# Moving VectorE work behind a copy, and re-dealing background steps, in a fused attention and two-MLP kernel

## The chip, the cores and the metric

The kernel runs on one core of a Trainium2 chip. The metric is device time in microseconds, as the median of several runs; lower is better.

## The reference

Eight batches (B = 8) of eight heads, 576 rows of 64, go through a packed attention: 32 packed queries p attend to k and v, and then q attends to the packed result, which serves as key and value.

```
s = scale * q @ k.T ; a = exp(s - max(s)) ; a = a / (sum(a) + 1e-9) ; out = a @ v
p_packed = attention(p, k, v)
out      = attention(q, p_packed, p_packed)
x = out as 4608 x 512
x = silu(x @ w_in1) @ w_out1            # 512 -> 2048 -> 512
x = (h * clip(h + 3, 0, 6) / 6) @ w_out2, h = x @ w_in2
```

All is float32 at the ends. Products are made exact enough by splitting each operand in a high and a low part (gh and gl, a2h and a2l, and so on) and adding three products.

## The kernel before, in words

The 4608 tokens are worked in NBLK = 9 blocks of 512: blocks 0 to 7 hold the first 512 rows of each batch, block 8 the 64-row tails of all eight. `block` (L985) runs the first MLP on one block: for each of 16 slices f of the inner dimension it calls `hidden` (L937: the products into hps, then Silu on ScalarE), `split_g` (L963: gh on ScalarE, gl on VectorE), and `projects(f - 2)` (L997 and L970: 12 products into four accumulators). Blocks 0 and 8 are fat: their hidden part has 12 products per f; in the others the attention's value product is folded into the weights and it has 6. After the ninth block a second MLP (`Second`, L1056) works on everything.

**The attention is threaded between these products.** Half a batch (four heads) is a quad n; 16 quads. A `window(c, d, b, a, ...)` (L823) lists steps for four quads in different stages: c is in its first softmax's scores, d in its second softmax's, b is c of the window before, a is d of the window before. `Plan` (L753) holds the steps with a place in the block, a list of needs and a wait in ticks; a tick is one matmul of the MLP. `tick` runs, between products, each step whose place has come and whose needs are met, in the order of places. Every engine carries out its instructions in the order in which they are issued, and so does the DMA queue of SyncE.

The steps that matter here, in the order of places in a window:

- `exps` (L834) and `ends` (L839) of the window before: the two exponentials on ScalarE, and after them `post1(b)` (L459, the reciprocal of the first softmax's sum) and `post2(a)` (L562, four VectorE instructions L566 to L569: sum, add, reciprocal, multiply of the second softmax's weights).
- `t`: `step_kpq` (L398) transposes the first softmax's weights of b and the tails of k and q on TensorE and copies them out: a1 by ScalarE, a1Tt and qtT by VectorE (L111 is the helper's line), kp by ScalarE.
- `pp` (L489; L466 has the products): the first softmax's weights times v. It reads a1 (L472) and a1Tt (L475). In block 1 it is a step of its own, 6 ticks or more after `t`; later it is part of the score step.
- `q0, q1, k0, k1` (`turn`, L859; `step_tr`, L442): from quad 4 on each is one VectorE transpose (L446) of a loaded tile nat. They need nothing of the `t` step. The second of each pair calls `use`, which may issue the next loads.
- `u` (L571 and L580): VectorE transposes the scaled weights (L573, and the tails, L585) and splits them.
- the score step (`step_zs`, L508): L514 reads q, L518 reads k, L608 reads the tails. It also ends the use of v, upon which the loads of the next v, q and k are issued.

Block 1 has the windows (c, d) = (4, -), (5, -), (6, 4), (7, 5), and a closing window without new quads. A window is named here by this pair; b = 5 and a = none in (6, 4), b = 6 and a = 4 in (7, 5), b = 7 and a = 5 in the closing one. Blocks 2 to 5 have two windows with quads and a closing one; block 6 none with a new c; block 7 none.

**Preparation.** Beside this, `Prep` (L269) turns the second MLP's weights into seven combinations in DRAM, in 32 units of nine steps after six empty ones (L313 to L343). A unit's stages: two ScalarE passes over the loaded tile praw (L180, L186), two VectorE passes (L195, L199) with the load of the next unit's tile issued a step later (L289, L291), a GpSimd add (L324), four VectorE sums (L327 to L330), two ScalarE copies (L332, L333), two GpSimd subtractions (L335, L336) and, with the next unit's first step, three stores on SyncE's queue (L340 to L342). `nxt` (L1879) runs the steps. It is called with full = True after `split_g` and at the end of an f, and with full = False in the middle of the projects (from f = 2 on) and, in a fat block, in the middle of the hidden part. In blocks 1 to 6 a call with full = True runs one step and one with False none; in block 7 (j == B - 1) two and one; in block 8 one and none.

```
1889    for _ in range(1 + full if j == B - 1 else full):
1890        prep.step()
```

Of the kernel before, what the change touches and what calls it, by code (L numbers as in the profile page):

```python
# [18 lines left out]
def tile_pack_attention_two_mlps(ctx: ExitStack, tc, q, k, v, p, w_in1, w_out1, w_in2, w_out2, out):  # L19
# [9 lines left out]
    B, H, S, D = q.shape  # L29
# [368 lines left out]
    def step_kpq(c, d, b, p=None, x=None):  # L398

        if b is not None:  # L400
            d1, _ = st.pop(("d1", b))
            rows = bank()
            for i in range(NI):
                nc.tensor.transpose(rows[:, i * P:(i + 1) * P], d1[:, i * P:(i + 1) * P], ident)
        ps = bank()
        if b is not None:
            nc.tensor.transpose(ps[0:TAIL, 3 * P:], d1[:, T:S], ident)
        if p is not None:
            step_pt(p)
        if x is not None:  # L410
            step_xt(x, ps[:, 3 * P:])
        if c is not None:
            nc.tensor.transpose(ps[:, 0:P], pair(st.pop(("pbd", c)), 0), ident)
        for a, what, n in (1, "k", c), (2, "q", d):
            for j in range(2 if n is not None else 0):
                o = a * P + j * TAIL
                nc.tensor.transpose(ps[:, o:o + TAIL], pair(nat[what, n], j), ident[0:TAIL, 0:TAIL])
            if n is not None:
                del nat[what, n]
        if b is not None:  # L420
            st["a1", b] = half_kb(b, "T", 5)
            copy(out=st["a1", b], in_=rows)
            st["a1t", b] = at.tile([TAIL, P], F32, tag="a1Tt", name="a1Tt")
            copy_short(out=st["a1t", b], in_=ps[0:TAIL, 3 * P:])
        if p is not None:
            step_ptc(p)
        if c is not None:
            t = at.tile([P, 2 * P], F32, tag="kp", name="kp")
            copy(out=t, in_=ps[:, 0:2 * P])
            st["kp", c] = t  # L430
        if d is not None:
            t = at.tile([P, P], F32, tag="qtT", name="qtT")
            copy_short(out=t, in_=ps[:, 2 * P:3 * P])
            st["qt", d] = t
        if x is not None:
            step_xtc(x)
# [5 lines left out]
    def step_tr(n, what, j):  # L442
        m = nat.pop((what, n, j))
        if n >= 4:
            t = half_kb(n, "T", 5)
            nc.vector.transpose(out=t, in_=m)  # L446
            st[what, n, j] = t
            return
        ps = bank()
        turn_rows(ps, m)  # L450
        t = half_kb(n, "T", 5)
        copy(out=t, in_=ps)
        st[what, n, j] = t
# [260 lines left out]
    for j in range(2, B - 1):  # L714
        c, d = QPB * (j + 2), QPB * (j + 1)
# [107 lines left out]
    def window(c, d, b, a, j, x):  # L823
# [4 lines left out]
        before = ("exps", b, a), ("ends", b, a)  # L828

        def add(n, what, cost, fn, *need, tile=None, bank=5, also=(), count=1):  # L830
            if n is not None:
                steps.append(((what, n), cost, fn, need, tile, bank, [k for k in also if k[1] is not None], count))
# [4 lines left out]
                    fn(n)  # L837

        def ends():  # L839
            for n, fn in (c, post1), (d, post2):  # L840
                if n is not None:
                    fn(n)

        def kpq():
            step_kpq(c, d, b)
            if c is not None:
                load_p_after(c)

# [6 lines left out]
        if ends_block:  # L855
            a = None
        add(c, "spread", 0, lambda: spread_p(c), ("kpq", b), bank=0)

        def turn():  # L859
            add(d, "q0", 0, lambda: step_tr(d, "q", 0), bank=0, tile=("z", d))  # L860
            add(d, "q1", 0, lambda: [step_tr(d, "q", 1), use("q", d)], ("q0", d), bank=0, tile=("z", d))
            add(a, "u", 0, lambda: [step_u(a), step_ut(a)], before[1], bank=8)
            add(c, "k0", 0, lambda: step_tr(c, "k", 0), (("q1", d), 0), bank=0, tile=("s", c))
            add(c, "k1", 0, lambda: [step_tr(c, "k", 1), use("k", c)], ("k0", c), bank=0, tile=("s", c))

# [13 lines left out]
        else:  # L879
# [2 lines left out]

            def transposes():
                step_kpq(c, d, b, p0, x)
                if c is not None:
                    load_p_after(c)

# [30 lines left out]
        steps.append((("ends", c, d), 0, ends, (("exps", c, d),), None, 0, (), 1))  # L918
        return steps

    pend = []

    WAIT = {"spread": 8, "kpq": 7, "q0": 6, "q1": 8, "k0": 6, "k1": 8, "t": 8, "tt": 8, "pp": 9, "pt": 6, "z": 4, "zt": 10, "s": 4, "st": 7,
            "exps": 22, "ends": 18, "u": 14, "split": 10, "xt": 12}
# [905 lines left out]
    for j in range(NBLK):  # L1830
# [46 lines left out]
        calls = [0]  # L1877

        def nxt(f, full, j=j):  # L1879
            if j == 0:  # L1880
                if full:
                    feed.advance()
                    calls[0] += 1
                    if 20 <= calls[0] < 25:
                        next_in()
                else:
                    feed.begin()
            else:
                for _ in range(1 + full if j == B - 1 else full):
                    prep.step()  # L1890
                if full and j == B:
                    mlp2.begin_step()

        def boundary(j=j):
            if j < B - 1:
                n = QPB * (j + 2) - 1
                plan.finish(lambda key: key[0] == "ends" and key[2] == n)
                step_u(n)
                step_ut(n)
            elif j == B - 1:  # L1900
                for c in range(KC):
                    split_x(c, xf[c])
# [44 lines left out]
```

## Time and profile before

| | |
|---|---|
| runs | 1529.72, 1538.01, 1539.9 us; median 1538.01 |
| profiled execution | 1529.94 us, its span 1528.1 us, mean granted TensorE clock 0.996 |
| TensorE matmul | 1482.3 us busy, 97% of the span |
| VectorE, ScalarE, GpSimd | 1034.6, 778.8, 190.8 us busy |
| blocks 0, 1, 7, 8 of the first MLP | 151.8, 110.8, 76.5, 85.6 us |
| blocks 2 to 6 together | 406.3 us |
| second MLP | 697.1 us |

A block is measured from the last copy of the block before's accumulators (L1028) to its own. PE is TensorE, PEld its weight loads, DVE VectorE, ACT ScalarE, POOL GpSimd, SP SyncE; SPq is its DMA queue. A matmul's recorded duration is longer than its distance to the next, since matmuls overlap; distances are taken from starts. In brackets at the end of a timeline row stands the idle time of the engine just before it and what ended it.

### The profile page before, as it was taken

What the parts mean: (1) busy time and instruction counts of PE and PEld (TensorE: products, weight loads), DVE (VectorE), ACT (ScalarE), POOL (GpSimd) and SP (SyncE); (2) the same over time, 40 slices, a digit from 0 to 9 for tenths busy, and PEclk for the clock granted to TensorE, in tenths of its full rate; (3) what the DMA queues carried; (4) which work ended last, traced back from release to release, by engine and by line L of the source; (5) the groups of instructions that cost most, each with busy time, mean ns of one, the idle gap of its engine ahead of it and who ended that gap; (6) DMA issues with size and microseconds to landing.
All of it is one profiled execution on the core that took longest, in us unless ns stands there. A gap on an engine that the chain in (4) does not pass through costs nothing.

```text
span 1528.1 us, 21726 instructions
## 1 busy us (share of the span) xinstructions
PE 1482.3 (97%) x7550; PEld 1229.2 (80%) x7550; DVE 1034.6 (68%) x1695; ACT 778.8 (51%) x1241; POOL 190.8 (12%) x177
## 2 busy tenths in 40 slices
PE   7999978999999999999999999999999999999998
PEld 4777756777777777777788888888888888999998
DVE  6767456765576656644452768877887787878777
ACT  6876646655575466555442334433443344444442
POOL 2433101111211211124220000000000000000000
PEclk9999999999999999999999999999999999999999
DMA  9998788978598759859893667677767766897887
GB/s 246 313 308 283 217 220 229 276 210 226 158 261 249 204 140 318 241 162 270 239 285 120 195 207 233 194 221 235 234 193 221 233 218 209 282 315 253 271 274 222
DMA packets 434509, 358.52 MB, mean 235 GB/s; under 512 B 191200, under 2 KB 325856, under 8 KB 434400
## 3 DMA queue, kind: packets, MB, share of 16 engines
q1 hardware_dynamic: 423632, 343.79, 76.0%
q10 hardware_dynamic: 10768, 13.34, 2.7%
q8 instruction: 61, 1.00, 0.3%
q14 instruction: 48, 0.39, 0.1%
HBM read 295.17 MB, written 61.87 MB: 234 GB/s over the span
## 4 chain that ended last, share of the span: by engine, by line
PE 81%; DMA 6%; DVE 4%; ACT 4%; SPq 2%; issue 1%; POOL 1%; ACTq 0%; POOLq 0%; DVEq 0%
PE b L1223 8%; PE b L1224 8%; PE b L1222 8%; PE b L1317 7%; PE b L1320 7%; PE b L1319 7%; PE acc L974 7%; PE acc L975 7%; PE acc L976 7%; PE hps L951 4%; PE hps L953 4%; PE hps L952 4%; DMA nat<-in_k_dram 1%; DMA w1i<-win 1%; DMA wi<-w1i 1%
## 5 line engine op out<-in xcount | busy, mean ns | idle before, releaser
L967 DVE TENSOR_TENSOR gl<-hps,gh 128x512 fp32r<-128x512 f32 x144 | 98.8, 686 | 173.8 <-ACT gh L966 173.4
L1319 PE MATMUL b<-ro,ws 128*128 128x512 f32 (+2 forms) x564 | 206.2, 366 | 0.0
L1320 PE MATMUL b<-ro,ws 128*128 128x512 f32 (+2 forms) x564 | 206.2, 366 | 0.0
L1222 PE MATMUL b<-xc,ws 128*128 128x512 f32 (+1 forms) x560 | 205.6, 367 | 0.0
L1224 PE MATMUL b<-xc,ws 128*128 128x512 f32 (+1 forms) x560 | 205.6, 367 | 0.0
L1223 PE MATMUL b<-xc,ws 128*128 128x512 f32 (+1 forms) x560 | 205.5, 367 | 0.0
L1265 DVE TENSOR_TENSOR ro<-g,ro 128x1024 fp32r<-128x1024 f32 (+1 forms) x140 | 161.3, 1157 | 41.6 <-ACT ro L1260 41.3
L1260 ACT CAST ro<-g 128x1024 fp32r<-128x1024 f32 (+1 forms) x140 | 132.0, 967 | 93.3 <-DVE g L1253 33.3
L1317 PE MATMUL b<-ro,ws 128*128 128x512 f32 (+2 forms) x564 | 138.9, 367 | 0.3
L959 ACT ACTIVATE hps<-hps 128x512 f32<-128x512 f32 x144 | 84.2, 584 | 99.7 <-PE hps L953 98.9
L974 PE MATMUL acc<-gh,wo 128*128 128x512 f32 x288 | 116.1, 403 | 2.8 <-ACT gh L966 2.8
L1319 PEld LDWEIGHTS b<-ro,ws 128*128 128x128 f32 x564 | 105.9, 188 | 13.2
L1320 PEld LDWEIGHTS b<-ro,ws 128*128 128x128 f32 x564 | 105.9, 188 | 13.1
L1222 PEld LDWEIGHTS b<-xc,ws 128*128 128x128 f32 x560 | 105.1, 188 | 13.3
L1223 PEld LDWEIGHTS b<-xc,ws 128*128 128x128 f32 x560 | 105.1, 188 | 13.2
L1224 PEld LDWEIGHTS b<-xc,ws 128*128 128x128 f32 x560 | 105.1, 188 | 13.0
L974 PE MATMUL acc<-gh,wr 128*128 128x512 f32 x288 | 113.7, 395 | 1.8 <-ACT gh L966 1.8
L1317 PEld LDWEIGHTS b<-ro,ws 128*128 128x128 f32 x564 | 102.9, 188 | 15.1 <-DVE ro L1265 2.2
L975 PE MATMUL acc<-gl,wo 128*128 128x512 f32 x288 | 113.7, 395 | 0.6 <-DVE gl L967 0.4
L976 PE MATMUL acc<-gh,wo 128*128 128x512 f32 x288 | 113.4, 394 | 0.0
L975 PE MATMUL acc<-gl,wr 128*128 128x512 f32 x288 | 112.7, 391 | 0.5 <-DVE gl L967 0.4
L976 PE MATMUL acc<-gh,wr 128*128 128x512 f32 x288 | 112.4, 390 | 0.0
(310 smaller groups left out, 2887.5 us busy)
## 6 DMA issues: line engine op xcount, KB each, us to landing
ws<-w2in SPq DMA_DIRECT2D x280, 256.0 KB, 3.3
ws<-w2out SPq DMA_DIRECT2D x280, 256.0 KB, 3.4
wi<-w1i SPq DMA_DIRECT2D x80, 512.0 KB, 6.2
wo<-w1o SPq DMA_DIRECT2D x64, 512.0 KB, 5.8
x1d<-x SPq DMA_DIRECT2D x18, 512.0 KB, 5.3
w1i<-win SPq DMA_DIRECT2D x16, 512.0 KB, 6.4
praw<-in_moe_w_in_dram SPq DMA_DIRECT2D x32, 256.0 KB, 5.5
praw<-in_moe_w_out_dram SPq DMA_DIRECT2D x32, 256.0 KB, 5.8
```

What stands on the lines that cost most here:

```text
L967: nc.vector.tensor_sub(out=gl, in0=g, in1=f32(gh))
L974: mm(acc[e], lhsT=w[:, 0, s], rhs=gh, start=first, stop=False)
L975: mm(acc[e], lhsT=w[:, 0, s], rhs=gl, start=False, stop=False)
L976: mm(acc[e], lhsT=w[:, 1, s], rhs=gh, start=False, stop=last)
L1222: mm(ps, lhsT=wh, rhs=xs[k][:, 0, c], start=first, stop=False, skip_group_check=True)
L1223: mm(ps, lhsT=wh, rhs=xs[k][:, 1, c], start=False, stop=False, skip_group_check=True)
L1224: mm(ps, lhsT=wl, rhs=xs[k][:, 0, c], start=False, stop=last, skip_group_check=True)
L1260: nc.scalar.copy(out=t[:, 0], in_=v)
L1265: nc.vector.tensor_sub(out=t[:, 1], in0=self.operand(s), in1=f32(t[:, 0]))
L1317: mm(to, lhsT=wh, rhs=x, start=False, stop=last, skip_group_check=True)
L1319: mm(to, lhsT=wh, rhs=x, start=first, stop=False, skip_group_check=True)
L1320: mm(to, lhsT=wl, rhs=x, start=False, stop=False, skip_group_check=True)
```

## The change

Three things. The transposes of q and k in block 1 also need `t` of the same window (in other blocks the added need names a step that does not exist and is always met). `ends` no longer scales the second softmax's weights where the window has a c: it notes d in the list `after_t`, and `weigh` scales what is noted, at the end of `t`'s own work, or at once where there is no c, or at the block's boundary before u; u needs `t` as well. And a call of `nxt` in blocks 7 and 8 runs one preparation step whatever full is, in block 7 every sixth call two; in blocks 1 to 6 nothing changes there.

```diff
         def ends():
-            for n, fn in (c, post1), (d, post2):
-                if n is not None:
-                    fn(n)
+            if c is not None:
+                post1(c)
+            if d is not None:
+                after_t.append(d)
+            if c is None:
+                weigh()
 
         def kpq():
             step_kpq(c, d, b)
+            weigh()
...
         def turn():
-            add(d, "q0", 0, lambda: step_tr(d, "q", 0), bank=0, tile=("z", d))
+            add(d, "q0", 0, lambda: step_tr(d, "q", 0), (("t", b if j == 1 else None), 0), bank=0, tile=("z", d))
             add(d, "q1", 0, lambda: [step_tr(d, "q", 1), use("q", d)], ("q0", d), bank=0, tile=("z", d))
-            add(a, "u", 0, lambda: [step_u(a), step_ut(a)], before[1], bank=8)
+            add(a, "u", 0, lambda: [step_u(a), step_ut(a)], before[1], (("t", b), 0), bank=8)
             add(c, "k0", 0, lambda: step_tr(c, "k", 0), (("q1", d), 0), bank=0, tile=("s", c))
...
             def transposes():
                 step_kpq(c, d, b, p0, x)
+                weigh()
...
-    pend = []
+    pend, after_t = [], []
+
+    def weigh():
+        while after_t:
+            post2(after_t.pop(0))
...
             else:
-                for _ in range(1 + full if j == B - 1 else full):
+                calls[0] += 1
+                for _ in range(1 + (j == B - 1 and calls[0] % 6 == 0) if j >= B - 1 else full):
                     prep.step()
...
                 plan.finish(lambda key: key[0] == "ends" and key[2] == n)
+                weigh()
                 step_u(n)
```

## Rows read from the trace of the kernel before

**Rows 1.** Page: the chain of waits, shares of the span by engine.

```profile
PE 81%; DMA 6%; DVE 4%; ACT 4%; SPq 2%; issue 1%; POOL 1%; ACTq 0%; POOLq 0%; DVEq 0%
```

**Rows 2.** Busy time by stretch: blocks 1, 2 to 6, 7, 8; length, engines, clock, DMA.

```profile
151.80:262.60 110.80, 98.47 (x600) 74.89 (x599) 58.34 (x127) 59.90 (x100) 13.99 (x17) 0.98 0.79 216
262.60:668.90 406.30, 400.48 (x2142) 316.12 (x2141) 263.64 (x534) 244.80 (x415) 68.20 (x67) 1.00 0.79 222
668.90:745.40 76.50, 70.81 (x294) 55.26 (x293) 33.73 (x73) 42.02 (x74) 32.43 (x27) 0.98 0.92 247
745.40:831.00 85.60, 85.60 (x379) 70.87 (x378) 30.61 (x45) 31.88 (x51) 11.26 (x8) 1.00 0.73 219
```

**Rows 3.** Timeline of TensorE, block 1: start, duration, line, operation, tiles, count, idle.

```profile
173.11 0.32 PE L475 MATMUL abank<-vt,a1Tt 64*32 64x64 f32 x8 [1.09 <-DVE a1Tt L111]
...
196.58 0.44 PE L475 MATMUL abank<-vt,a1Tt 64*32 64x64 f32 x8 [4.49 <-DVE a1Tt L111]
196.95 0.80 PE L974 MATMUL acc<-gh,wo 128*128 128x512 f32 x1
...
199.68 0.45 PE L951 MATMUL hps<-a2h,fused 128*128 128x512 f32 x1
...
225.30 0.32 PE L475 MATMUL abank<-vt,a1Tt 64*32 64x64 f32 x8 [2.71 <-DVE a1Tt L111]
...
232.84 0.39 PE L608 MATMUL abank<-tails,ppf 128*128 128x128 f32 x2
...
249.18 0.32 PE L475 MATMUL abank<-vt,a1Tt 64*32 64x64 f32 x8 [1.86 <-DVE a1Tt L111]
```

**Rows 4.** Busy time by stretch, behind the stop at 196.58.

```profile
196.60:200.00 3.40, 3.40 (x16) 2.60 (x17) 1.46 (x4) 1.46 (x3) 0.00 (x0) 0.53 0.88 309
```

**Rows 5.** Timeline of VectorE in window (6, 4).

```profile
192.07 0.71 DVE L446 STREAM_TRANSPOSE T<-nat 128x512 f32<-128x512 f32 x1 [2.25 <-DMA nat<-in_q_dram]
...
196.26 0.26 DVE L111 COPY a1Tt<-abank 64x128 f32<-64x128 f32 x1
...
197.64 0.71 DVE L446 STREAM_TRANSPOSE T<-nat 128x512 f32<-128x512 f32 x1 [0.38 <-DMA nat<-in_k_dram]
```

**Rows 6.** Timeline of VectorE in window (7, 5).

```profile
221.56 0.71 DVE L446 STREAM_TRANSPOSE T<-nat 128x512 f32<-128x512 f32 x1 [1.51 <-DMA nat<-in_k_dram]
...
223.02 0.73 DVE L566 TENSOR_REDUCE s2s<-d 128x18 f32<-128x576 f32 x1
...
224.97 0.28 DVE L111 COPY a1Tt<-abank 64x128 f32<-64x128 f32 x1
...
228.39 0.49 DVE L585 STREAM_TRANSPOSE tails<-d 64x64 f32<-64x64 f32 x2
```

**Rows 7.** Timeline of VectorE in the closing window of block 1.

```profile
246.87 0.97 DVE L567 TENSOR_SCALAR s2s<-s2s 128x18 f32<-128x18 f32 x1
```

**Rows 8.** TensorE's waits in block 7: us in total, times, longest.

```profile
PE acc L974 <- ACT gh L966: 4.6, 4, 2.6
```

**Rows 9.** ScalarE's waits in block 7.

```profile
ACT hi L332 <- POOL c L324: 16.0, 8, 3.3
ACT pr L180 <- DMA praw<-in_moe_w_out_dram: 10.9, 4, 4.0
```

**Rows 10.** ScalarE's longest wait in block 8.

```profile
ACT hps L959 <- PE hps L953: 36.3, 13, 4.2
```

**Rows 11.** Timeline of SyncE's queue, the loads of q for window (7, 5).

```profile
206.96 7.25 SPq L373 DMA_DIRECT2D nat<-in_q_dram  x8
```

**Rows 12.** Timeline of ScalarE, gh in window (7, 5).

```profile
220.82 0.59 ACT L966 CAST gh<-hps 128x512 fp32r<-128x512 f32 x1
```

**Rows 13.** TensorE's waits for a1Tt in blocks 2 to 6.

```profile
PE abank L475 <- DVE a1Tt L111: 0.8, 1, 0.8
```

**Rows 14.** Page: DMA issues, preparation's loads: count, KB each, us to landing.

```profile
praw<-in_moe_w_out_dram SPq DMA_DIRECT2D x32, 256.0 KB, 5.8
```

**Rows 15.** Waits of SyncE's queue in block 7.

```profile
SPq L340 <- ACT hi L333: 27.8, 6, 14.4
```

## The prediction

> **What bounds the kernel now.** I read the chain of waits first: TensorE holds 81% of it, every other engine or queue 6% or less [rows 1]. So time can only come from places where TensorE stands still or runs slowly, and the next view is the busy time by stretch, block by block [rows 2]. The reader is to compare the length of a stretch with TensorE's busy time in it. Block 8 has no idle time: 85.60 us for 379 matmuls, 0.226 us each. Blocks 2 to 6 lose 5.8 us in 406. Block 1 loses 12.3 us in 110.8, and block 7, with less to multiply than block 8, loses most per microsecond: 294 matmuls at block 8's 0.226 us are 66.4 us, and the block takes 76.5, so 10.1 us are lost (5.7 idle, the rest matmuls that run slower around the stops). These two blocks are the ones that the change works on.
>
> In block 1 TensorE stops at one instruction, L475, which multiplies by the copied tail of the first softmax's weights (a1Tt): 1.09, 4.49, 2.71 and 1.86 us in its four windows [rows 3]. After the long stop the granted clock is 0.53, the lower of its two levels (1.2 of 2.4 GHz), for 3.4 us [rows 4]. VectorE's rows say why a1Tt is late. In window (6,4) VectorE sits in front of transposes of q and k whose data are still under way (2.25 us at 192.07) and copies a1Tt only at 196.26, behind them [rows 5]. In window (7,5) the same transposes end at 222.27, and then the second softmax's scaling (L566 to L569) runs from 223.02 to 224.97, ahead of the copy [rows 6]. In the closing window the scaling alone stands there [rows 7].
>
> In block 7 TensorE waits for gh, a ScalarE product, 4.6 us in four stops [rows 8]. ScalarE is late because the preparation's steps block it: it waits 10.9 us for the preparation's loads, up to 4.0 at a time, and 16.0 us for GpSimd's add [rows 9]. In block 8, where the preparation runs at two steps per f, ScalarE instead waits 36.3 us for TensorE [rows 10]: it has time to spare.
>
> **The change part by part.** *Transposes of q and k in block 1.* They now need the step t of the same window. That binds in windows (6,4) and (7,5) alone, since the others have no q. Four L446 of 0.71 us each [rows 5] move behind t's copies, with the two calls that may issue loads. Those calls issue nothing where they stand: the next loads wait for v, released in the score step, and the queue spends 7.25 us on q's eight transfers alone after that [rows 11]. So nothing moves on SP's queue or POOL's.
>
> Window (6,4): t's matmuls stay where they are, and VectorE goes from gl straight to a1Tt. What is left of the 4.49 us lies between 0 and 1.09, the stop in the window that has neither transposes nor scaling in front [rows 3]; gl, which waits for ScalarE, still stands ahead of the copy, so I take 0.4. Gain 4.1. The slow stretch goes too: from 196.95 to 199.68 six matmuls take 2.73 us [rows 3], 1.36 at 0.226; gain 1.4. Together 5.5 (4.8 to 5.9). Behind the moved transposes queue the next gl, the value product's scaling and the splits of fused weights. The last transpose starts at 197.64 because its data land then [rows 5]; without the stop the scores come some 5.5 us before their old place, still just after it. I charge nothing here; if that cover is gone, the score step waits, which is a rival below.
>
> Window (7,5): 2.71 falls to 0.5 by the same bounds, gain 2.2 (1.6 to 2.7). Here something is late next: step u, whose tails end at 228.88 [rows 6] and are read by L608 at 232.84 [rows 3]. With VectorE free for gl at 221.41, when gh ends [rows 12], and not when the k transpose lets go, and with four transposes (2.8 us) in front, they end near 228.9 - 0.8 + 2.8 = 230.9; L608 will want them near 230.6. I charge 0.5 (0 to 2.0). Net 1.7 (-0.4 to 2.7).
>
> *The scaling behind the copies.* It is off the path until u. In the closing window 1.86 us go; the work behind the copy (scaling, value, u, splits into block 2) is as long as before and ends hardly sooner, so I keep 1.2 (0 to 1.86). Block 1 in all 8.4 (4.4 to 10.5). In block 0 the copies are ScalarE's, and windows without a next k scale where they did: nothing. In blocks 2 to 6 one stop of 0.8 us at L475 is all there is to win [rows 13]: 0.6 (0 to 0.8). The new wait of u for t adds nothing, since u already waits 18 ticks behind the ends step that comes before t.
>
> One row speaks against moving the scaling: its 18-element L567 took 0.97 us in the closing window, half of the 1.95 us that the whole group took in the window before [rows 6, 7]. The Trainium skill (SBUF — State Buffer, Who interferes with whom) says that VectorE and GpSimd share one port pair which an instruction holds to its end, so a moved scaling that meets a preparation add waits for all of it. By that rule the sum would be smaller by one such wait of 0.8 us, in window (7,5), 16.7 instead of 17.5. The row agrees with a wait of this kind but does not name GpSimd.
>
> *Preparation.* Calls per block are counted from the code: in block 7, 46 (two for each of the first two f, then three), before 32 x 2 + 14 x 1 = 78 steps, now 46 + 7 = 53; in block 8, before 32, now 62. Blocks 1 to 6 give 192 either way, and all units need 295. So before 25 steps were left for block 8, now 50; both end near its f = 12. About 2.8 units of nine steps leave block 7, with their loads, ScalarE passes, GpSimd adds and stores. In block 7 a unit's load and its first use are six steps apart: before a little over one f (4.1 us at 18 matmuls), now two f, 8.2 us, against 5.8 us from issue to landing [rows 14]. So ScalarE's wait for loads should vanish, and with at most one of a unit's chained stages in most f the 16.0 us behind GpSimd shrink. Of 10.1 us I take 9.0 back (5 if the start of the block, with stores and loads crowded, stays as it is; 10.1 at most).
>
> Block 8 takes 25 more steps. Priced as in block 7, 10.1 / 78 = 0.13 us each, they would cost 3.3 us; hidden they cost nothing. I take 0.5, nearest the row of this block itself: 36.3 us of ScalarE waiting and no TensorE idle time [rows 2, 10]. DMA there rises from 219 GB/s (18.7 MB) by 2.8 x 1.4 MB (512 KB in and 896 out per unit, by the code) to some 267 GB/s, share 0.89 by proportion, below block 7's 0.92 [rows 2].
>
> **Sum.** 8.4 + 0.6 + 9.0 - 0.5 = 17.5 us (6 to 21.4). The profiled execution took 1529.94 us, so 1512.4 (1508.5 to 1524). The median of the runs shown is 1538.01, 8.1 above it, and no row tells where the 8.1 lie; halfway between 1512.4 and 1520.5 I predict 1516.
>
> **Rivals.** *A: block 7 goes on stopping*, because the loads are late through traffic and not through spacing (DMA share 0.92 there [rows 2]). For it: the first stops would stand at the block's start, where stores of block 6 land too. Against: blocks 2 to 6 run the same chain at two steps per f with hardly a stop. Then only 8.5 us go: about 1521 in the profile. Chance 0.11. *B: the wait moves to the scores.* The transposes come late, L514 and L518 stop instead of L475, and block 1 gives nothing: 1529.9 - 9.1 = 1521. For it: k's last data in window (6,4) land at 197.64 [rows 5] whatever the order. Against: the scores come after that. Chance 0.11. *C: slower, by block 8.* SP's queue is in order; in block 7 a preparation store at its head waited up to 14.4 us for ScalarE [rows 15]. If stores of the five units now in block 8 hold the weights' loads back like this, TensorE waits for wi. With five tiles a load has some four f of 5.4 us, so it decides only from a delay of about 15 us on; 1.1 us in each of the 16 f eats the gain, 2.2 us gives 35 - 17 = 18 us slower, 1548. Against: ScalarE is rarely late in block 8 [rows 10]. Chance 0.06. *D: the change does not bind*: if t is emitted early anyway, order stays as it was; but the rows show the copies last in all three windows. Chance 0.02, 1538.
>
> **Numbers.** The forecast has 0.70. 1% (15.4 us; about what a measurement of this kernel can tell from no change) lies inside its spread: I put 0.53 of it on faster by over 1% and 0.17 within. A and B give 0.05 faster and 0.17 within, C 0.05 slower and 0.01 within, D 0.02 within; 0.58, 0.37, 0.05. The range runs from 1507 to 1531: the sum's upper end below, A and B with the runs' 8.1 us above.
>
> **What would show it.** Right: L475's stops in block 1 under 1 us each, a1Tt ahead of L566 and of the L446 pair, no stretch at a granted clock near 0.5 there; block 7 near 67 us with ScalarE's wait for praw near nothing; block 8 still at 0.226 us per matmul. Wrong: stops at L514, L518 or L608 in windows (6,4) and (7,5); gh still late in block 7; TensorE waiting for wi or gh in block 8.

## The result and the profile after

The changed kernel takes 1518.54 us (median of six runs, 1516.09 to 1520.86) beside 1535.12 for the kernel before (1529.72 to 1539.9): ratio 0.989, 95% interval 0.987 to 0.992. A second measurement gave 0.990 (0.988 to 0.991). The forecast was 1516. The profiled execution took 1516.09 us, its span 1514.3.

In the chain of waits TensorE's share is 86%, against 81% in [rows 1], and every other engine has 4% or less.

Busy time by stretch, in the columns of [rows 2]: block 1, blocks 2 to 6, block 7, block 8.

```profile
152.40:258.70 106.30, 99.48 (x597) 75.12 (x596) 57.31 (x126) 59.39 (x99) 14.01 (x17) 0.98 0.83 225
258.70:665.50 406.80, 401.30 (x2143) 316.39 (x2142) 264.72 (x534) 245.13 (x416) 68.25 (x67) 1.00 0.80 223
665.50:730.60 65.10, 65.10 (x290) 53.90 (x289) 28.29 (x59) 35.45 (x62) 21.77 (x18) 1.00 0.84 222
730.60:817.20 86.60, 86.60 (x384) 71.71 (x383) 38.04 (x60) 38.47 (x64) 23.84 (x17) 1.00 0.89 260
```

Against [rows 2]: block 1 is 4.5 us shorter, blocks 2 to 6 are 0.5 longer, block 7 is 11.4 shorter and block 8 1.0 longer. Block 0 is 0.6 longer, and the second MLP takes 697.1 us as before. In all 13.85 us.

**Block 7 has no idle time left.** ScalarE's waits there (us in total, times, longest) answer to [rows 9]: 16.0 us behind GpSimd's add and 10.9 for praw have become these.

```profile
ACT hi L332 <- POOL c L324: 0.7, 1, 0.7
ACT pr L180 <- DMA praw<-in_moe_w_out_dram: 0.6, 1, 0.6
```

Block 8's extra 1.0 is no slowing: it has 384 matmuls instead of 379, still at 0.226 us each, and block 7 has 290 instead of 294. The copy that makes the border was VectorE's before and ended at 745.37, 2 us behind block 8's first product; it now comes some four matmuls earlier. Blocks 7 and 8 together went from 162.1 to 151.7.

**In block 1 L475 waits in one window only, the one the change does not touch, and two other waits of about a microsecond or more have appeared.** Timeline of TensorE, as in [rows 3]. The first row is window (5, -). Lines from the f-loop on stand nine further down, so L974 is now L983.

```profile
173.72 0.32 PE L475 MATMUL abank<-vt,a1Tt 64*32 64x64 f32 x8 [1.08 <-DVE a1Tt L111]
...
192.72 0.32 PE L475 MATMUL abank<-vt,a1Tt 64*32 64x64 f32 x8
...
217.86 0.32 PE L475 MATMUL abank<-vt,a1Tt 64*32 64x64 f32 x8
...
225.97 0.64 PE L518 MATMUL abank<-T,kp 128*64 128x512 f32 x1 [0.95 <-DVE T L446]
...
241.78 0.32 PE L475 MATMUL abank<-vt,a1Tt 64*32 64x64 f32 x8
...
249.67 0.50 PE L983 MATMUL acc<-gh,wo 128*128 128x512 f32 x1 [2.40 <-DMA wo<-w1o]
```

TensorE's waits at L472 for ScalarE's copy a1, 2.1 us in three stops, are the same before and after.

VectorE's rows show the order that the change asked for. The first two are window (6, 4): the copy, and the last of the four transposes of q and k behind it, late with its data; compare [rows 5].

```profile
192.40 0.26 DVE L111 COPY a1Tt<-abank 64x128 f32<-64x128 f32 x1
...
199.29 0.71 DVE L446 STREAM_TRANSPOSE T<-nat 128x512 f32<-128x512 f32 x1 [3.57 <-DMA nat<-in_k_dram]
...
217.54 0.26 DVE L111 COPY a1Tt<-abank 64x128 f32<-64x128 f32 x1
...
218.45 0.74 DVE L566 TENSOR_REDUCE s2s<-d 128x18 f32<-128x576 f32 x1
...
222.75 0.69 DVE L573 STREAM_TRANSPOSE abank<-d 128x512 f32<-128x512 f32 x1
...
225.21 0.71 DVE L446 STREAM_TRANSPOSE T<-nat 128x512 f32<-128x512 f32 x1
```

The last four rows are window (7, 5): copy, then scaling, then u from 222.75. The last transpose of k comes at 225.21, behind u, and it is what L518 waits for at 225.97.

The second new wait is a load. SyncE's queue around it:

```profile
233.01 5.42 SPq L373 DMA_DIRECT2D nat<-in_q_dram  x8
238.53 5.33 SPq L373 DMA_DIRECT2D nat<-in_k_dram  x8
243.96 0.57 SPq L260 DMA_DIRECT2D wo<-w1o  x1
```

The load of wo is issued at 243.96, directly behind sixteen loads of q and k that hold the queue without a gap (in the trace of before it was issued at 244.50). TensorE now wants it at 247.27 and gets it at 249.67. Then the clock falls to its lower level for part of the next stretch (clock 0.62 in this row):

```profile
250.00:254.50 4.50, 4.50 (x14) 3.53 (x13) 0.43 (x1) 1.52 (x3) 0.00 (x0) 0.62 1.03 341
```

Fourteen matmuls at 0.226 us would be 3.2 us; they take 4.5.

### The profile page after: what moved, and what is told of

It reads as the page before. It is cut to its first block, busy times and chain, and to the rows that moved or that the text cites. A ratio compares the mean times of both kernels' runs of the same rounds, so it can differ in the third digit from the quotient of the medians.

```text
span 1514.3 us, 21726 instructions
## 1 busy us (share of the span) xinstructions
PE 1477.9 (98%) x7550; PEld 1227.8 (81%) x7550; DVE 1036.3 (68%) x1695; ACT 778.8 (51%) x1241; POOL 192.5 (13%) x177
## 4 chain that ended last, share of the span: by engine, by line
PE 86%; ACT 4%; DMA 4%; DVE 3%; issue 1%; SPq 1%; POOL 0%; ACTq 0%; DVEq 0%; POOLq 0%
PE b L1232 8%; PE b L1233 8%; PE b L1231 8%; PE b L1326 8%; PE acc L983 8%; PE b L1329 7%; PE b L1328 7%; PE acc L984 7%; PE acc L985 7%; PE hps L960 4%; PE hps L962 4%; PE hps L961 4%; PE abank L672 1%; DMA w1i<-win 1%; PE abank L674 1%
## 5 line engine op out<-in xcount | busy, mean ns | idle before, releaser
L968 ACT ACTIVATE hps<-hps 128x512 f32<-128x512 f32 x144 | 84.1, 584 | 97.5 <-PE hps L962 96.7
L983 PE MATMUL acc<-gh,wo 128*128 128x512 f32 x288 | 115.3, 400 | 2.4 <-DMA wo<-w1o 2.4
L983 PE MATMUL acc<-gh,wr 128*128 128x512 f32 x288 | 113.5, 394 | 0.0
```

The source lines that it names most:

```text
L983: mm(acc[e], lhsT=w[:, 0, s], rhs=gh, start=first, stop=False)
```

## The experiments

Each was profiled once and timed against the kernel before on the same chip. The ratio is taken over all runs; the lengths in us, by the same borders, are those of one execution:

| kernel | ratio (95%) | block 1 | block 2 | 3 to 6 | 7 | 8 |
|---|---|---|---|---|---|---|
| before | | 110.8 | 83.6 | 322.7 | 76.5 | 85.6 |
| changed | 0.989 (0.987 to 0.992) | 106.3 | 84.0 | 322.8 | 65.1 | 86.6 |
| after_again | 0.990 (0.988 to 0.991) | 107.3 | 84.1 | 324.7 | 65.2 | 86.5 |
| e1_prep_only | 0.993 (0.991 to 0.995) | 116.2 | 84.1 | 323.2 | 65.1 | 86.6 |
| e2_transposes_only | 0.996 (0.995 to 0.998) | 109.0 | 84.2 | 323.3 | 76.7 | 85.6 |
| e3_scaling_only | 0.995 (0.993 to 0.997) | 106.0 | 84.3 | 323.0 | 77.0 | 85.5 |
| e4_wo_scalar_queue | 0.990 (0.988 to 0.992) | 103.0 | 91.2 | 323.5 | 65.2 | 86.5 |
| e5_transposes_together | 0.988 (0.986 to 0.990) | 106.1 | 88.5 | 324.9 | 65.1 | 86.7 |
| e8_both | 0.988 (0.986 to 0.990) | 104.0 | 87.9 | 323.7 | 65.1 | 86.6 |
| e6_before_early_loads | 1.000 (0.999 to 1.002) | 112.1 | 83.6 | 323.6 | 77.8 | 84.0 |
| e7_loads_before_stores | 0.996 (0.994 to 0.997) | 115.5 | 86.8 | 322.6 | 69.9 | 85.7 |
| e9_prep_off_block1 | 0.997 (0.996 to 0.999) | 99.8 | 83.9 | 344.6 | 65.2 | 87.4 |
| e10_prep_off_wo_scalar | 0.998 (0.997 to 1.000) | 99.8 | 82.9 | 344.8 | 65.2 | 87.6 |
| e11_less_prep_in_block1 | 0.994 (0.992 to 0.995) | 101.3 | 90.7 | 336.0 | 63.7 | 86.5 |

### One part at a time

**The preparation alone** (the kernel before, with the two lines of the dealing).

```diff
-                for _ in range(1 + full if j == B - 1 else full):
+                calls[0] += 1
+                for _ in range(1 + (j == B - 1 and calls[0] % 6 == 0) if j >= B - 1 else full):
```

> The kernel before with the preparation's new dealing alone; block 1 as before. Theory (the three parts add, and most of the gain is block 7): blocks 7 and 8 come out as in the changed kernel, 65.1 and 86.6 us instead of 76.5 and 85.6, so about 10.4 us less than before, ratio about 0.993; block 1 stays at 110.8 with its stop of some 4.5 us at L475. Rival (the profile's 10.4 us in blocks 7 and 8 is partly an effect of block 1's work being moved, which hands other states of the preparation's units on): block 7 stays above 68 us, and the gain is 7 us or less.

Blocks 7 and 8 come out as in the changed kernel; that part stands by itself. Block 1, whose program is that of before, takes 116.2 us in this execution. The stops at L475 are the old ones (3.93, 3.41, 1.86 us). What differs is the clock: 0.93 over the block against 0.98 in [rows 2], with a slow stretch after each of the three stops.

```profile
154.60:270.80 116.20, 103.72 (x601) 78.81 (x600) 58.28 (x127) 60.02 (x101) 13.95 (x17) 0.93 0.76 207
...
255.00:260.00 5.00, 5.00 (x16) 3.91 (x13) 2.29 (x6) 1.31 (x3) 0.00 (x0) 0.50 0.04 14
```

The second row is the stretch after the closing window's stop: 16 matmuls in 5 us at clock 0.50. The profiled execution of before had one such stretch [rows 4]. Two more kernels below with block 1 as before took 112.1 and 115.5, at clocks 0.95 and 0.93. In these four executions TensorE's waits at that instruction sum to 9.2 to 10.3 us. So with about the same stops this block takes between 110.8 and 116.2 us, and the trace that the forecast was made from was the cheapest of the four.

**The transposes alone.**

```diff
-            add(d, "q0", 0, lambda: step_tr(d, "q", 0), bank=0, tile=("z", d))
+            add(d, "q0", 0, lambda: step_tr(d, "q", 0), (("t", b if j == 1 else None), 0), bank=0, tile=("z", d))
```

> The kernel before with q0's need of t in block 1 alone; scaling and preparation as before. Theory (the long stop in window (6,4) was the transposes standing ahead of the copy, the one in (7,5) mostly the scaling): the 4.49 us stop and the slow stretch behind it go, the stop in (7,5) stays near 2 us because the scaling still stands ahead of the copy there (it took 1.95 us), the closing window's 1.86 stays. Loads are issued as before, so part comes back as a stop for the first projects' weights (wo) near 249 us, 2.4 us in the changed kernel: net block 1 3 to 5 us shorter, ratio about 0.997. Rival (the scaling held the copy in both): stops at L475 stay above 3 us in sum in windows (6,4) and (7,5), and block 1 gains under 2 us.

TensorE at L475 in windows (6, 4), (7, 5) and the closing one:

```profile
197.97 0.32 PE L475 MATMUL abank<-vt,a1Tt 64*32 64x64 f32 x8
225.03 0.32 PE L475 MATMUL abank<-vt,a1Tt 64*32 64x64 f32 x8 [1.99 <-DVE a1Tt L111]
250.50 0.44 PE L475 MATMUL abank<-vt,a1Tt 64*32 64x64 f32 x8 [1.86 <-DVE a1Tt L111]
```

The theory held on the stops: the long one was the transposes, the next one mostly the scaling. Two details missed. Block 1 is 1.8 us shorter than in the trace of before and not 3 to 5 (under 2 was a sign of the rival); but both stops that are left are followed by a slow stretch here (clock 0.95 over the block), and by the ratio the part gains what was expected. And there is no stop for wo near 249; that the two stops which are left delay TensorE enough is the likely reason.

**The scaling alone** (the rest of the change in `window`: `after_t`, `weigh`, and u's need of t).

```diff
-            for n, fn in (c, post1), (d, post2):
-                if n is not None:
-                    fn(n)
+            if c is not None:
+                post1(c)
+            if d is not None:
+                after_t.append(d)
...
```

> The kernel before with the second softmax's scaling behind the copies alone; the transposes stand ahead of them as before. Theory: the 4.49 us stop in window (6,4) stays as it is (no scaling stands there), the stop in (7,5) falls from 2.71 to about 0.8 and the closing one from 1.86 to under 0.3, so 2 to 4 us less in block 1, ratio 0.998; no new stop for weights near 249 us, because TensorE still arrives some 4 us later there than in the changed kernel. Rival (the work behind the copies is as late as before and the wait moves to u's tails, L608, or to L518): block 1 within 1 us of 110.8.

```profile
198.05 0.32 PE L475 MATMUL abank<-vt,a1Tt 64*32 64x64 f32 x8 [3.79 <-DVE a1Tt L111]
224.42 0.32 PE L475 MATMUL abank<-vt,a1Tt 64*32 64x64 f32 x8 [0.19 <-DVE a1Tt L111]
246.37 0.32 PE L475 MATMUL abank<-vt,a1Tt 64*32 64x64 f32 x8
```

The stops came as expected, with a gain above the 2 to 4 us expected: block 1 takes 106.0 us with the long stop still in it, as little as with the whole change. What the moved transposes save on top of that is taken back. By the ratios the three parts alone give 0.7, 0.4 and 0.5%, 1.6% in sum, and together 1.1%. The gap is about as large as the intervals allow, and the two parts in block 1 are where the traces show an overlap.

### What takes it back in block 1

**The changed kernel again**, as the measure for the three kernels after it.

> The changed kernel once more, as the measure for the three kernels beside it: ratio to the kernel before 0.989 (0.987 to 0.992), block 1 near 106.3 us with a stop of 2.4 us for the weights wo near 249.7 us and one of 0.9 to 1.3 us at L518 in window (7,5). If that stop for wo is an accident of one execution, it is missing here.

Both new waits are there again:

```profile
229.10 0.64 PE L518 MATMUL abank<-T,kp 128*64 128x512 f32 x1 [0.95 <-DVE T L446]
253.34 0.80 PE L983 MATMUL acc<-gh,wo 128*128 128x512 f32 x1 [2.89 <-DMA wo<-w1o]
```

**The weights' load on another queue.**

```diff
-            nc.sync.dma_start(out=f32(t), in_=w1o[f].rearrange("n p f -> p n f"))
+            (nc.scalar if j == 1 else nc.sync).dma_start(out=f32(t), in_=w1o[f].rearrange("n p f -> p n f"))
```

> The changed kernel with block 1's loads of the projects' weights (wo, 8 transfers) issued on ScalarE's queue instead of SyncE's. Theory (block 1 is now held by the order and the issue of SyncE's queue, in which the load of wo stands behind two windows' loads of q, k and v): wo lands before it is wanted, the stop of 2.4 us near 249.7 and the slow stretch behind it (some 1.7 us) go, block 1 is about 102 to 103 us, 3 to 4 us less than in the changed kernel, ratio to the kernel before about 0.987. Rival (the DMA engines' bandwidth holds it; 225 GB/s and a share of 0.83 in the block): the wait moves to another load (nat, wi) and block 1 stays within 1 us of 106.3. Second rival (an issue on ScalarE's queue holds ScalarE's products up): gh late, block 1 longer.

Half right. On ScalarE's queue the load is issued at 230.8, the stop for wo goes and block 1 is 103.0, so its place behind the sixteen loads did hold it. But block 2 then takes 91.2 us, with a stop for wi:

```profile
285.19 0.77 PE L672 MATMUL abank<-wi,ph 128*128 128x512 f32 x1 [4.36 <-DMA wi<-w1i]
```

Blocks 1 and 2 together take 194.2 us, against 190.3 and 191.4 in the changed kernel's two executions, and the ratio is no better. The gain is not kept. That TensorE, earlier still, only meets the next late load is the likely reason but not shown: in e7_loads_before_stores, whose block 2 has the program of before, block 2 took 86.8 us with a stop of 3.38 us for wi, and there TensorE was not early.

**The four transposes directly behind one another.**

```diff
-            add(d, "q1", 0, lambda: [step_tr(d, "q", 1), use("q", d)], ("q0", d), bank=0, tile=("z", d))
+            add(d, "q1", 0, lambda: [step_tr(d, "q", 1), use("q", d)], (("q0", d), 0) if j == 1 else ("q0", d), bank=0, tile=("z", d))
```

(and k1 after k0 in the same way)

> The changed kernel with q1 directly behind q0 and k1 directly behind k0 in block 1 (without the wait of six products between them), so that the four transposes follow the copies at once and k's second one stands ahead of u. Theory (L518's stop in window (7,5), 0.95 to 1.32 us, is the second k transpose coming behind u's 2.4 us on VectorE): that stop goes, block 1 0.7 to 1.3 us shorter unless the weights' loads take it back near 249 us, in which case the stop there grows by as much and the block stays at 106.3. Rival: u, now later, is waited for at L608 and the time comes out the same.

```profile
226.69 0.34 PE L523 MATMUL abank<-qtT,ppT 128*64 128x64 f32 x4 [1.23 <-DVE a2l L577]
...
250.73 0.50 PE L983 MATMUL acc<-gh,wo 128*128 128x512 f32 x1 [3.17 <-DMA wo<-w1o]
```

The rival held, at another line than it named: u, now behind the transposes, delays L523 by 1.23 us, more than L518 had lost. The stop for wo is longer, and block 1 is the same. (This profile is the slowest of the kernel's five runs, 1523.49 us against a median of 1518.54, so its block 2 of 88.5 may belong to the execution.)

**Both edits.**

```diff
+            (nc.scalar if j == 1 else nc.sync).dma_start(out=f32(t), in_=w1o[f].rearrange("n p f -> p n f"))
...
+            add(d, "q1", 0, lambda: [step_tr(d, "q", 1), use("q", d)], (("q0", d), 0) if j == 1 else ("q0", d), bank=0, tile=("z", d))
...
```

> The changed kernel with both edits: wo on ScalarE's queue in block 1, and the transposes directly behind one another. Theory (the two costs are separate): block 1 near 101.5 us, 4.5 to 5 us less than the changed kernel, total about 1514, ratio to the kernel before 0.986. If SyncE's queue is not what holds wo back, no more than 1 us comes.

Block 1 takes 104.0 and block 2 87.9, not 101.5 and 84: the two do not add. The waits are those seen in each, 1.2 us at L523 in block 1 and 3.44 us for wi in block 2.

**The preparation out of block 1.** No step in block 1 and in the first eight f of block 2, a step in every call of blocks 3, 5 and 6.

```diff
-                for _ in range(1 + (j == B - 1 and calls[0] % 6 == 0) if j >= B - 1 else full):
+                n = full and (j > 2 or j == 2 and f >= 8) or j in (3, 5, 6)
+                for _ in range(1 + (j == B - 1 and calls[0] % 6 == 0) if j >= B - 1 else n):
```

> The changed kernel with no preparation step in block 1 and in the first eight f of block 2 (48 steps, some 5.3 units of 1.4 MB), and instead a step in every call in blocks 3, 5 and 6 (14 more each) and 6 more in block 8. Theory (block 1 and the first half of block 2 are held by traffic: DMA shares of 0.93 to 1.07 there, against 0.73 to 0.78 in blocks 3, 5 and 6): the stops for wo in block 1 (2.4 to 3.1 us) and for wi in block 2 (1.4 to 2.2) go, 3 to 7 us less in these blocks, ratio to the kernel before 0.985 to 0.987. Rival 1 (not traffic but the place in SyncE's queue behind 16 loads of q and k of 0.64 us each): the stops stay within 1 us of what they were, ratio 0.989 as before. Rival 2 (blocks 3, 5 and 6 now lose to the preparation what block 7 lost before): these blocks get longer by over 1 us each, and the ratio is 0.990 or more.

Block 1 falls to 99.8 us, and the stops for wo in it and for wi in block 2 go:

```profile
152.70:252.50 99.80, 98.39 (x601) 74.23 (x600) 51.16 (x110) 53.54 (x89) 3.41 (x8) 1.00 0.78 206
```

TensorE's waits for a1 in block 1, 2.1 us in the changed kernel, are nearly gone as well:

```profile
PE abank L472 <- ACT T L108: 0.3, 1, 0.3
```

So without the preparation beside it block 1 is 6.5 us shorter than in the changed kernel, and block 2 keeps its 83.9. Not all of this is gain that the change had lost. About 2.9 us are stops that the kernel before had too: the waits at L472, in front of which ScalarE makes the preparation's copies hi (L332, L333, from 239.62 in the changed kernel's closing window), and the 1.1 us at L475 in window (5, -). The rest, some 3.6 us, matches the stop for wo and the slow stretch behind it. But the second rival came true as well, and outweighs it: block 3 takes 82.9 us instead of 78.9, block 5 96.5 instead of 78.9, and block 6 80.3 instead of 79.0. ScalarE's longest wait in block 5, and SyncE's queue ahead of one such wait:

```profile
ACT pr L180 <- DMA praw<-in_moe_w_in_dram: 22.9, 2, 14.6
```

```profile
566.35 5.37 SPq L373 DMA_DIRECT2D nat<-in_q_dram  x8
...
572.96 1.00 SPq L291 DMA_DIRECT2D praw<-in_moe_w_in_dram  x2
```

```profile
583.93 0.48 PE L494 MATMUL abank<-ident,ppf 128*128 128x128 f32 x1 [8.20 <-DVE ppf L486]
```

At the denser pace a load of praw falls behind a window's loads of q. ScalarE stands at its pass over praw until 579.26, with the attention's work and gh behind it, and TensorE stops for 8.20 us.

**The same with wo on ScalarE's queue.**

```diff
+            (nc.scalar if j == 1 else nc.sync).dma_start(out=f32(t), in_=w1o[f].rearrange("n p f -> p n f"))
...
+                n = full and (j > 2 or j == 2 and f >= 8) or j in (3, 5, 6)
```

> The same with wo's eight loads of block 1 on ScalarE's queue. Moved alone, they took 3.3 to 4.3 us off block 1, and block 2 gave 7 back in stops for wi. Theory (traffic): with the preparation's 7.5 MB out of the way block 1 is near 102 us and block 2 stays at 84, ratio to the kernel before about 0.984. Rival (block 2's stops for wi come from the order of SyncE's queue): block 2 is again 88 us or longer, ratio 0.988 to 0.990.

Blocks 1 and 2 take 99.8 and 82.9: without the preparation's transfers in the way, wo's queue makes no difference in block 1. The losses in blocks 3 and 5 are those of the run before.

### What block 7 lost its time to

**Loads issued three steps earlier** (the kernel before, 78 steps in block 7).

```diff
                 conv_begin(key, self.room)
+                if 20 <= u and u + 1 < len(self.units):
+                    self.load(u + 1)
...
-                if u + 1 < len(self.units):
+                if u < 20:
                     self.load(u + 1)
```

> The kernel before, with its 78 preparation steps in block 7, but from the 21st unit on the next unit's tile praw is loaded in the unit's first step, nine steps ahead of its first use instead of six. It tells apart why block 7 got shorter: loads late by their spacing in steps, or too much of a unit's chain in one f. Theory of the prediction (both count, the spacing for 10.9 us and the wait behind GpSimd for 16.0 us of ScalarE's waiting): ScalarE's wait for praw in block 7 falls from 10.9 us to under 2, its wait behind GpSimd's add stays near 16, and block 7 gives back 3 to 6 of its 10.1 lost us. Rival 1 (traffic: the transfers themselves are late, DMA share 0.92): the wait for praw stays above 6 us and block 7 above 74 us. Rival 2 (the spacing was all of it): block 7 falls to 67 us or less with three preparation steps an f.

My theory fell, and what rival 1 (traffic) expected came: ScalarE's wait for praw in block 7 is as long as in [rows 9], and the block is no shorter.

```profile
ACT pr L180 <- DMA praw<-in_moe_w_out_dram: 12.2, 5, 6.1
```

SyncE's queue shows another reason than traffic, which the next run puts to the test. In the order of the program the load now stands three steps earlier, but directly behind the three stores of the unit before, and these wait for its last copies.

```profile
682.25 0.43 SPq L342 DMA_DIRECT2D w2out<-hi  x1
682.78 3.01 SPq L343 DMA_DIRECT2D w2out<-c  x1
...
687.02 3.91 SPq L289 DMA_DIRECT2D praw<-in_moe_w_out_dram  x2
```

**Loads ahead of the stores**, in the same step.

```diff
-                if u + 1 < len(self.units):
+                if u < 20:
                     self.load(u + 1)
...
+                if 19 <= u and u + 2 < len(self.units):
+                    self.load(u + 2)
                 to = w2[kind][f].rearrange("s p f -> p s f")
                 nc.sync.dma_start(out=to[:, :, h * P:(h + 1) * P], in_=hi)
```

> The kernel before (78 preparation steps in block 7), with the loads of praw from the 22nd unit on put directly ahead of the three stores of the unit two before, on the same queue; in the last experiment they stood in the same step directly behind these stores, and ScalarE's wait for praw stayed at 12.2 us. Theory now (SyncE's queue is in order, the stores wait for a unit's last ScalarE and GpSimd work, and the load of the next unit behind them is held with them): ScalarE's wait for praw in block 7 falls under 3 us, the wait behind GpSimd's add (15 to 16 us) stays, block 7 falls from 76.5 to about 70 to 74 us. Rival 1 (traffic: the transfers take as long wherever they are issued): the wait for praw stays above 8 us and block 7 at 76 to 78. Rival 2 (the chain of one unit's stages on ScalarE, VectorE and GpSimd is the whole cost): the wait for praw goes but the wait behind GpSimd grows by as much, and the block stays at 75 us or more.

```profile
679.20:749.10 69.90, 68.26 (x294) 55.83 (x293) 33.49 (x73) 41.58 (x74) 32.46 (x27) 0.98 1.03 270
```

```profile
ACT hi L332 <- POOL c L324: 15.0, 7, 3.2
...
ACT pr L180 <- DMA praw<-in_moe_w_out_dram: 3.7, 1, 3.7
```

ScalarE's wait for praw is 3.7 us instead of the under 3 expected, and the rest came as the theory had it. With all 78 steps, block 7 takes 69.9 us; 6.6 of its 10.1 lost us come back although DMA moves more per second (270 GB/s, share 1.03) than in [rows 2]. So neither traffic nor GpSimd was the main cost. ScalarE still waits 15.0 us for GpSimd's add, and that costs at most the 3.5 us that are left. What mostly stopped TensorE was the load of praw behind stores that wait: a loop from a unit's copies through its stores to the next unit's load. Between this run and the last only the order on the queue differs, and blocks 7 and 8 together take 155.6 us against 161.8 (162.1 before). The Trainium skill (DMA: Bandwidth & Descriptors, Anatomy of one DMA — SWDGE (gpsimd) path) says, in its section on GpSimd's path, that a DMA's wait for a semaphore is sat out by the issuing sequencer, not by the DMA engines; on SyncE's queue the pair of runs agrees with that.

**A version from all this**: the changed kernel without preparation from the seventh f of block 1 on, its 20 steps in blocks 7 and 8, and from block 7 on the loads ahead of the stores, as above.

```diff
-                for _ in range(1 + (j == B - 1 and calls[0] % 6 == 0) if j >= B - 1 else full):
+                n = full and not (j == 1 and f >= 6)
+                for _ in range(1 + (j == B - 1 and calls[0] % 3 == 0) if j >= B - 1 else n):
...
```

> The changed kernel with no preparation step from the seventh f of block 1 on (20 steps, some 2.2 units, 3.1 MB), these steps put into block 7 (every third call two instead of every sixth, 61 steps instead of 53) and block 8 (62 instead of 50), and with the loads of praw ahead of the stores from block 7 on. Theory (the preparation's transfers hold block 1; blocks 7 and 8 have room for a step in every call): block 1 falls from 106.3 or 107.3 to about 101 to 103, block 2 stays at 84, block 7 is 65 to 66.5 and block 8 87 to 87.5: 3 to 5 us less than the changed kernel, ratio to the kernel before 0.986 to 0.988. Rival (block 2 takes the gain back, as when wo's loads were moved, because block 2's own traffic of q, k and wi is what holds it): blocks 1 and 2 together within 1.5 us of 190.3 to 191.4, ratio 0.989 or more.

Blocks 1, 7 and 8 do what the theory says or better: 101.3, 63.7 and 86.5 us, with 20 more steps in the last two. The run is slower than the changed kernel for a reason neither theory had: blocks 2 and 4 take 90.7 and 96.3 us. They run one step per full call as ever, but the units are 20 steps further back, so they meet the windows in another phase. That this is the reason is read from the traces; no run moves the phase alone. In block 4 ScalarE waits for praw, whose load came behind k's, and TensorE then stops for 4.27 us at 465.40 for an exponential of ScalarE's:

```profile
460.74 0.66 ACT L180 ACTIVATE pr<-praw 128x512 f32<-128x512 f32 x1 [7.62 <-DMA praw<-in_moe_w_in_dram]
```

```profile
444.51 7.23 SPq L375 DMA_DIRECT2D nat<-in_k_dram  x8
...
452.93 0.94 SPq L291 DMA_DIRECT2D praw<-in_moe_w_in_dram  x2
```

No version beats the changed kernel by more than the intervals; e5_transposes_together and e8_both equal it.

## Why the prediction was right, and where it was not

**Block 7** (9.0 of 10.1 us to come back): all of it came back. The borders moved with it, so the sum over blocks 7 and 8 is the fair reading: 10.4 us against 8.5 forecast. The reason given was half wrong. It said the loads were late by their six steps of spacing; three steps more did nothing, and with the loads ahead of the stores 6.6 us came back at the old pace. How the thinner dealing gets the same is argued, not shown by a run of its own: a unit of nine steps now has 11.1 us (65.1 x 9 / 53) instead of 8.8, and the loop through the queue has time to close. The traces fit: the first of the three stores still waits 18.1 us for ScalarE's copies, but 5.4 at most against 27.8 and 14.4 before [rows 15], and the wait for praw is 0.6. The price of GpSimd's add, 16.0 us of ScalarE's waiting, was overrated as a cost of TensorE's time. Rival A (traffic) is out.

**Block 8** (0.5 to pay): nothing to pay, and the DMA share is the 0.89 that was worked out. Rival C saw that waiting stores hold the queue, but for the wrong load: no stop for wi in block 8, while praw in block 7 was held that way already before the change.

**Block 1** (8.4 us): the mechanism was right and the size was off. All that the forecast put on L475 came: 4.49, 2.71 and 1.86 us and the slow stretch behind the first, 10.4 us, the upper end of its bounds. What it did not have is what is late next. Taking the starts of the same product in both kernels, TensorE leads its old place by 5.8 us behind window (6, 4) and by 8.1 behind L475 in (7, 5). Over the score step there the lead falls to 6.1. It is 8.0 in the closing window, 5.4 behind the load of wo and 3.8 at the end of the slow stretch; after_again shows the same up to wo. So the step that waits for k's second transpose costs 2.0 us, more than the 0.95 that its row shows as idle. From L514 to the MLP's next product it takes 2.41 us before and 4.42 after:

```profile
230.57 1.08 PE L514 MATMUL abank<-T,ppT 128*64 128x512 f32 x4
...
232.98 0.47 PE L951 MATMUL hps<-a2h,fused 128*128 128x512 f32 x1
```

```profile
223.09 1.08 PE L514 MATMUL abank<-T,ppT 128*64 128x512 f32 x4
...
227.51 0.48 PE L960 MATMUL hps<-a2h,fused 128*128 128x512 f32 x1
```

The forecast charged 0.5 us for u at L608, where nothing waits; in fact L518 waits, because q1 and k1 still keep their six products' wait and u slips in between. And it said of SP's queue that nothing moves on it. True, and just this is the larger of the mis-sized terms: with the loads issued when they were before and TensorE eight us ahead of its old place, the wait for wo takes 2.6 us and the slow clock behind it 1.7. Another 0.4 goes in the score step of window (6, 4). Together some 6.7 of the 10.4 us go back, which leaves 3.8 by the starts of products; by the borders it is 4.5, since the copies at the end of the block also come 0.7 us sooner behind the last product. Rival B expected a wait at L514 or L518 in place of L475 and nothing gained; the wait at L518 came, at 2.0 us. By the forecast's own signs, a stop at L518 stood under wrong, and under right stood no slow stretch in block 1: one is left, behind wo and not behind L475.

**The runs.** The profile gained 13.85 us and the medians 16.6. The forecast could not say where the 8.1 us between the profiled execution and the median lay. The runs with block 1 as before show it in part: 110.8, 112.1, 115.5 and 116.2 us for the same program, mean 113.7, against 106.3 and 107.3, mean 106.8, with the change. By these means the change takes some 6.9 us from block 1, because with the stops their slow stretches go too. Block 0, which none of the four edits concerned touches, differs as well: 151.8 us in the profile of before, 153.6 to 157.6 in e1, e2, e6 and e7. So that 1516 came so near to 1518.54 is partly luck: block 1's term was too large against its own trace by 3.9 us, and half of the 8.1, added without a row for it, stood for a loss that the change partly removes.

**Blocks 2 to 6** (0.6 to gain): 0.5 lost. The 0.8 us stop at L475 is gone, and a stop of 0.94 us has appeared in block 4 (L672, for a2l of u). The scaling alone shows the same stop (0.93 us), so it belongs to that part. How far the order of VectorE's work could avoid it was not tried.

**The moved scaling and GpSimd.** In the closing window L567 takes 0.79 us (0.97 before), and in window (7, 5) 0.18. The rows of VectorE and GpSimd:

```profile
219.22 0.18 DVE L567 TENSOR_SCALAR s2s<-s2s 128x18 f32<-128x18 f32 x1
...
241.58 0.79 DVE L567 TENSOR_SCALAR s2s<-s2s 128x18 f32<-128x18 f32 x1
```

```profile
240.79 1.55 POOL L336 TENSOR_TENSOR c<-c,hi 128x640 fp32r<-128x640 f32 x1
```

The long one ends at 242.37, where GpSimd's subtraction ends (242.34); GpSimd does nothing beside the short one. In the trace of before the long one of [rows 7] ends at 247.84, and GpSimd's L336 beside it runs from 246.26 to 247.80. This agrees with the rule of the port pair that the forecast took from the Trainium skill, and it cost nothing here, since the copy now stands ahead of it. The 16.7 by that rule instead of 17.5 were a wait in window (7, 5) that did not occur.

For wo in block 1 its place on SyncE's queue is shown as the cause by the run that moves it. Open is whether DMA bandwidth or the queue holds wi in block 2: leaving the preparation out takes away both, 1.4 MB and five transfers a unit.

## What to carry to other kernels

When a stop is removed, look for the load that TensorE will reach earlier, and at its place in the queue: work that is not moved can become late by what is won. On an in-order queue put a load that an engine will wait for ahead of stores that wait for that engine; here the order was worth 6.6 us and three steps of lead nothing. Background work that shares an engine and a queue with a periodic foreground has a phase: in the one run that left out 20 steps in block 1, blocks 2 and 4 were 6.7 and 10.3 us longer than in the changed kernel, at the same pace. So time the whole kernel and not the block. And compare several executions of the unchanged program, stretch by stretch, before sizing a gain from one profile.

## What had not been expected of the hardware

Stops of TensorE of like length in the same place were followed by a stretch at the lower clock level in some executions and not in others: over the five us behind the closing window's 1.86 us the granted clock was 0.50 in the run of the preparation alone (its row stands above), and 1.00 in the trace of before:

```profile
249.50:254.50 5.00, 5.00 (x23) 4.04 (x24) 3.70 (x9) 3.02 (x6) 0.13 (x1) 1.00 0.64 230
```

Sixteen matmuls fit in the one and 23 in the other. Why the clock fell in the one and not in the other is not shown. The four executions of this block differ by up to 5.4 us with the program unchanged.
